# Prelude buffers of a recurrence-and-routing kernel kept to the end, early rows gathered in the prelude, and the first expert search moved

## The chip, the cores and the metric

The kernel runs on one core of a Trainium2 chip. Times are device microseconds (us) of one execution. The kernel before took 1211.76 us as the median of 3 runs (1211.62 to 1213.09). The engines are named as in the profile: PE (matrix products; PEld are its weight loads), DVE (vector engine), ACT (activation engine), POOL (general-purpose engine, which also issues indirect DMAs) and SP (which issues most plain DMAs here).

## The reference, cut to what matters

A gated linear recurrence runs over four sequences of 5056 tokens with 256 channels; its output, 20224 tokens in all, goes through a mixture of 8 experts in which every expert takes exactly N / E = 2528 tokens. Which token goes where is decided greedily over all (token, expert) logits from the largest down.

```python
f = lower_bound + (1 - lower_bound) * sigmoid(f_logit)
h = 0
for t in range(S):
    h = f[:, t] * h + (1 - f[:, t]) * x[:, t]
    y[:, t] = h
x = y.reshape(N, D)                    # N 20224, D 256
logits = x @ w_gate                    # E 8
counts, assigned = zeros(E), -ones(N)
for tok, e in pairs_by_falling_logit(logits):
    if assigned[tok] < 0 and counts[e] < N // E:
        assigned[tok] = e
        counts[e] += 1
for e in range(E):
    m = assigned == e
    out[m] = maximum(x[m] @ w1[e], 0) @ w2[e]     # F 1024
```

## The kernel before, in words

The 20224 tokens are 158 tiles of 128. The program has two stages that share the on-chip memory.

The prelude (lines 147 to 817) takes the tokens in 40 chunks of four tiles (the last has two). For chunk i, `load` (line 161) has SP fetch f_logit and x into tiles `fl` and `xl`; each has four buffers, so a load waits until the chunk four before it has been read. `sig` has ACT form the sigmoid and POOL multiply it with x. `fwd` transposes both on PE (`pf`, `pb`), ACT makes the gate `fg`, DVE runs the scan `g`. `back` (line 714) makes four products `pr` of 264 columns from g with `iw`, a matrix that holds the identity and the gate's weights: 256 columns are the row of the token, 8 its logits. A `pr` tile is one of four PSUM banks and is copied to `hr` by DVE or ACT in turn; POOL copies the logits into `X`. `store` (line 733) has SP write hr (264 columns a token) to `hbuf` in DRAM. `hr` is a ring of 22 buffers; inside the loop a store is issued for every second chunk, at most 18, and the rest when the loads are over.

While the chunks run, `prep` (line 737) finds each token's best expert from X: maximum M, comparison TMP, its product with the numbers `kc`, maximum A, one-hot O; and it forms an integer key K of M and the first-level masks MK of the later search, by comparing K with `thr0_f`. For the first 72 tiles (CE) this is done in three pieces; when it is done, `early` (line 580) estimates from them which expert certainly has 896 rows (EARLY) among these tiles, has POOL load that expert's weights, and lists the ids of those rows. Each step of `early` that needs PE takes a `pr` tile of its own (`ppr.tile`).

The second stage (`moe`, line 912) runs slots -1, 0, ..., 7. Slot -1 is the early expert's first 1920 rows, in chunks of 4, 3, 4 and 4 blocks of 128 rows. For each chunk POOL gathers the rows (`xg <- hbuf, ids`), PE transposes them (`pt`), ACT and DVE split them into a high and a low part (`xh`, `xl`); the weights are split likewise (`w1h`, `w1l`, `w2s`). `first` multiplies one of eight column groups of w1 (six products `pw`), ACT and DVE take hh and hl from it, and `second` multiplies them with w2s (twelve products `py`). ACT copies y, POOL scatters it to `out_dram`. A name that appears twice is meant by its operands: `xl <- fl, xl` is the prelude's product on POOL, `xl <- pt, xh` the low part of gathered rows on DVE.

Between these products the routing runs: `further` lists the other 1024 rows of slot -1, `search` finds a threshold in eight levels, `assign` and `compact` make the lists of the next expert. A planner (class Pace, lines 26 to 100) holds a cost for each operation and fixes at build time in which order the pieces go into PE's, DVE's and ACT's programs; each engine then works its program in order. Helper calls record every operation at line 100, so nearly all rows of the profile have L100 and are told apart by their names; SP's loads have L168 and its stores L735.

The prelude's pools are closed before `moe` opens its own (lines 923 to 938), so that a tile of `moe` lies where prelude tiles lay: one that lies over ring buffers waits until their stores have landed. The order of the pools there (gp for gathered rows, wa1, yp, xp, hp, wb, a gap of 8 KB, wa2) decides which tile lies over which ring buffer: here the first `xl` of gathered rows lies over those of chunks 29 and 31, the second hh over that of chunk 37, the first hl over that of chunk 39.

## Time and profile before

| what | value |
|---|---|
| median of 3 runs | 1211.76 us |
| the profiled execution's own time | 1210.67 us |
| its span, from the first instruction to the last | 1208.9 us |
| mean granted TensorE clock | 0.982 |
| PE busy | 1153.3 us, 95% of the span |
| DVE, ACT, POOL busy | 793.4, 539.0, 461.3 us |
| bytes moved by DMA | 125.25 MB |

A row of a timeline gives the start, the length, the engine, the operation, output and inputs, and in brackets how long the engine had stood idle before it and what ended that. A row of windows gives for a stretch the busy time of PE, PEld, DVE, ACT and POOL (in brackets how many instructions), the granted TensorE clock as a share of full speed, the mean busy share of the DMA engines and the GB/s they moved.

### The profile page before, as it was taken

The numbers are of one execution on the slowest core, as the hardware profiler recorded it, in microseconds if no ns is written. First come the engines' busy times: TensorE is split into PE (matmuls) and PEld (weight loads), VectorE is DVE, ScalarE is ACT, GpSimd is POOL, SyncE is SP. The second block draws the span as 40 slices with busy tenths as digits, with TensorE's granted clock in tenths as the row PEclk, the third lists the DMA queues.
The fourth block names the chain that finished last, engine by engine and source line by source line (L and its number), as shares of the span: only waits on it lengthen the run. The fifth ranks groups of instructions, "written<-read, shape, count | busy, mean of one in ns | idle before, by whom it ended". The sixth has DMA issues, their size and how long they took to land.

```text
span 1208.9 us, 22553 instructions
## 1 busy us (share of the span) xinstructions
PE 1153.3 (95%) x8821; PEld 1048.4 (87%) x8821; DVE 793.4 (66%) x1917; ACT 539.0 (45%) x1104; POOL 461.3 (38%) x459
## 2 busy tenths in 40 slices
PE   7898876998999999999999999999999999999997
PEld 7898865887888988899988988898889989999997
DVE  6998675678767867687887887967744542243221
ACT  7886762326325333643444354222554642253232
POOL 6676560332433333333433433333433333333322
PEclk9999987998999999999999999999999999999999
DMA  9999995112113112211311221111311311131110
GB/s 360 358 330 316 318 334 173 37 54 79 56 49 101 53 41 75 80 48 37 109 48 41 92 63 40 45 41 38 121 45 44 111 47 45 61 106 44 40 35 31
DMA packets 52447, 125.25 MB, mean 104 GB/s; under 512 B 8064, under 2 KB 28288, under 8 KB 51184
## 3 DMA queue, kind: packets, MB, share of 16 engines
q0 software_dynamic: 19248, 60.96, 15.6%
q1 hardware_dynamic: 32544, 62.78, 15.2%
q8 instruction: 71, 1.16, 0.4%
q14 instruction: 40, 0.33, 0.1%
q10 hardware_dynamic: 544, 0.01, 0.0%
HBM read 81.69 MB, written 42.10 MB: 102 GB/s over the span
## 4 chain that ended last, share of the span: by engine, by line
PE 80%; DMA 3%; issue 3%; DVE 1%; POOL 1%; ACT 0%; POOLq 0%; DVEq 0%; SPq 0%; ACTq 0%
PE py L100 37%; PE pw L100 35%; PE rt L100 4%; PE pt L100 2%; DMA hbuf<-hr 1%; PE pr L100 1%; DMA xg<-hbuf,ids 1%; DMA r<-in_moe_w_dram,wi 1%; PE pf L100 1%; PE pb L100 0%; POOL xg L100 0%; POOL out_dram L100 0%; DVE g L100 0%; ACT hh L100 0%; DVE hl L100 0%
## 5 line engine op out<-in xcount | busy, mean ns | idle before, releaser
L100 PE MATMUL py<-w2s,hh 128*128 128x256 f32 x2560 | 490.8, 288 | 0.5 <-ACT y L100 0.5
L100 ACT ACTIVATE hh<-pw 128x512 fp32r<-128x512 f32 (+3 forms) x328 | 191.2, 583 | 553.1 <-PE pw L100 470.8
L100 PEld LDWEIGHTS py<-w2s,hh 128*128 128x128 f32 x2560 | 409.3, 190 | 16.3 <-ACT y L100 0.7
L100 DVE SCALAR_TENSOR_TENSOR hl<-pw,hh 128x512 fp32r<-128x512 f32 (+3 forms) x328 | 219.6, 670 | 232.8 <-ACT hh L100 228.0
L100 PE MATMUL py<-w2s,hl 128*128 128x256 f32 (+1 forms) x1280 | 362.1, 283 | 0.0
L100 POOL DMA_INDIRECT out_dram<-y,ids x160 | 165.1, 1032 | 340.1 <-ACT hh L100 279.9
L100 POOL DMA_INDIRECT xg<-hbuf,ids x160 | 163.6, 1023 | 295.6 <-ACT hh L100 235.9
L100 PE MATMUL pw<-xh,w1h 128*128 128x512 f32 (+3 forms) x656 | 258.3, 394 | 4.7 <-DVE hl L100 4.7
L100 PE MATMUL pw<-xl,w1h 128*128 128x512 f32 (+3 forms) x656 | 259.1, 395 | 0.0
L100 PE MATMUL pw<-xh,w1l 128*128 128x512 f32 (+3 forms) x656 | 256.3, 391 | 0.0
L100 PEld LDWEIGHTS py<-w2s,hl 128*128 128x128 f32 (+1 forms) x1280 | 242.8, 190 | 0.0
L100 PEld LDWEIGHTS pw<-xh,w1l 128*128 128x128 f32 x656 | 124.8, 190 | 22.3
L100 PEld LDWEIGHTS pw<-xh,w1h 128*128 128x128 f32 x656 | 125.6, 191 | 17.2 <-DVE hl L100 5.1
L100 PEld LDWEIGHTS pw<-xl,w1h 128*128 128x128 f32 x656 | 125.6, 191 | 11.3 <-DVE xl L100 0.3
L100 POOL TENSOR_TENSOR xl<-fl,xl 128x1024 f32<-128x1024 f32 (+2 forms) x40 | 92.5, 2312 | 47.1 <-ACT fl L100 36.8
L100 DVE TENSOR_TENSOR_SCAN g<-fg,g,pb 128x512 f32<-128x512 f32 (+4 forms) x78 | 92.9, 1228 | 15.9 <-ACT fg L100 10.7
L100 PE MATMUL pr<-iw,g 128*128 128x136 f32 x632 | 81.8, 281 | 5.6 <-DVE hr L100 5.6
L100 PEld LDWEIGHTS pr<-iw,g 128*128 128x128 f32 x632 | 76.7, 191 | 7.0 <-DVE hr L100 6.8
L100 ACT ACTIVATE junk<-rt,r 128x158 bf16<-128x158 f32 (+1 forms) x153 | 59.4, 389 | 17.3 <-DVE r L100 14.4
L100 DVE TENSOR_TENSOR xl<-pt,xh 128x512 fp32r<-128x512 f32 (+2 forms) x81 | 54.2, 670 | 16.9 <-DMA hbuf<-hr 13.4
L100 PEld LDWEIGHTS pt<-identr,xg 128*128 128x128 f32 x320 | 36.4, 141 | 31.6 <-DVE xl L100 11.5
L100 ACT ACTIVATE fg<-pf,one,nomlb 128x512 f32<-128x512 f32 (+1 forms) x80 | 57.6, 769 | 7.3 <-PE pf L100 5.4
(213 smaller groups left out, 1189.1 us busy)
## 6 DMA issues: line engine op xcount, KB each, us to landing
hbuf<-hr SPq DMA_DIRECT2D x39, 528.0 KB, 9.3
fl<-in_f_logit_dram SPq DMA_DIRECT2D x38, 512.0 KB, 6.4
xl<-in_x_dram SPq DMA_DIRECT2D x38, 512.0 KB, 6.8
xg<-hbuf,ids POOLq DMA_INDIRECT x160, 2.8
out_dram<-y,ids POOLq DMA_INDIRECT x160, 2.4
fl<-in_f_logit_dram SPq DMA_DIRECT2D x3, 256.0 KB, 4.2
xl<-in_x_dram SPq DMA_DIRECT2D x3, 256.0 KB, 4.4
r<-in_moe_w_dram,wi POOLq DMA_INDIRECT x27, 5.5
```

The costliest lines, as they stand in the source:

```text
L100: r = f(*args, **kw)
```

## The change

- The pool of `fl` and `xl` is opened before the prelude's other pools and stays open to the end. A `fl` buffer is now 1056 columns wide (4 rows of 264) instead of 1024; the 32 more columns are zeroed once. In `moe` the `fl` buffers take the place of `gp` and hold gathered rows, the `xl` buffers take the place of `wa1` and hold the split w1 of slot -1 and of the odd slots.
- At the loop's step NCH - 2 the prelude issues the gathers of slot -1's first four blocks; ACT writes the four pieces of its w1h at steps NCH - 2 to NCH. The first of these gathers waits for two of the semaphores of plain DMAs, DMAHW2 and DMAHW5, as the first gather of the kernel before does.
- `early` no longer takes a `pr` tile. `back` gets a job, and the job's products are written into the columns behind 264 of the bank of the chunk's last product. The counts per expert are made by nine products of O with a matrix of ones; the lists are made in pieces of two blocks. `early` has to end inside the loop.
- Keys and first-level masks leave `prep`: the keys are formed for all tiles at once at the search's start, the masks in its first level. `prep` of the tiles up to 136 (CP) now stands inside the loop, and for tiles 72 to 104 the product with kc goes to POOL.
- The bound of 18 stores inside the loop is gone (19 now stand there). The pools of `moe` stand in another order, the gap is gone, and there are 13 y tiles instead of 3.

```diff
-    pre = ExitStack()
-    pin = pre.enter_context(tc.tile_pool(name="pin", bufs=LA))
+    pin = ctx.enter_context(tc.tile_pool(name="pin", bufs=LA))
+    pre = ExitStack()
...
     def early(wi, ids):
-            v.tensor_reduce(CR, O[:, :CE].rearrange("p c e -> p e c"), AX.X, OP.add)
-        yield 'PE'
-        ps = ppr.tile([P, 512], F32, name="pr")
-        nc.tensor.matmul(ps[:, :E], ones_r, CR, start=True, stop=True)
+        def sums(ps):
+            for g in range(CE // 8):
+                nc.tensor.matmul(ps[:, :64], ones_b, O[:, 8 * g:8 * g + 8].rearrange("p c e -> p (c e)"), start=(g == 0),
+                                 stop=(g == CE // 8 - 1))
+        yield sums
+        ps = beside[0]
...
-    def back(i):
+    def back(i, job=None):
...
-            pr = ppr.tile([P, 512], F32, name="pr")[:, :ROW]
+            pr = ppr.tile([P, 512], F32, name="pr")
+            mine = job is not None and k == n - 1
+            if mine:
+                beside[:] = [pr[:, ROW:]]
+                job(beside[0])
+            pr = pr[:, :ROW]
...
     def prep(c0, c1):
-        mb, k1 = m_.bitcast(I32), K1[:, c0:e]
-        far = v if c0 >= CE else nc.gpsimd
+        far = nc.gpsimd if c1 <= 128 else v
...
-        masks(half(K1, 1), thr0_f, c0, c1)
-        yield 'k'
...
+        if i >= NCH - 2:
+            if i < NCH:
+                WSE.append(pin.tile([P, FB, P], F32R, name="xl"))
...
+        if i == NCH - 2:
+            assert stored * KT >= CE
+            XGE = rows_tile(F32R)
+            for q in range(KT):
+                nc.gpsimd.indirect_dma_start(out=XGE[:, q * ROW:(q + 1) * ROW].bitcast(F32), out_offset=None,
+                                             in_=hbuf[:CE * P],
...
-    gp = pool("gp", 3)
-    wa1 = pool("wa1", 1)
-    YB = 3
+    wa2 = pool("wa2", 1)
+    YB = 13
     yp = pool("yp", YB)
+    wb_ = pool("wb", 1)
+    hp = pool("hp", 5)
     xp = pool("xp", 2)
-    hp = pool("hp", 5)
-    wb_ = pool("wb", 1)
-    gap = pool("gap", 1)
...
-    gather(*order[0])
-    issue(4)
+    XG[-1, 0] = g["XGE"].rearrange("p (q r) -> p q r", q=4)
```

PE's program in the middle of the prelude, where `early` has its places; pf, pb and pr are the chunk's products, g_1663 is the 0/1 matrix that picks rows, RAE the list's source, tri and nsub constants:

```order
 L100 MATMUL pf<-ident,fl 128x128 x8
 L100 MATMUL pb<-ident,xl 128x128 x8
-L100 MATMUL pr<-iw,g 128x136 x8
-L100 LDWEIGHTS g_1663
-L100 MATMUL pr<-RAE,g_1663 128x74
+L100 MATMUL pr<-iw,g 128x136 x6
+L100 LDWEIGHTS tri
+L100 MATMUL pr<-ecnt,tri 128x1
+L100 LDWEIGHTS nsub
+L100 MATMUL pr<-RSE,nsub 128x74
+L100 MATMUL pr<-iw,g 128x136 x2
```

Before, the estimate's products stood behind a chunk's eight in a bank of their own; now they stand between the chunk's third and fourth product, in the fourth one's bank.

ACT's program at the border of the two stages, with the semaphores that each row waits for (DMAHW: plain DMAs, DMASW: indirect ones), first before and then after the change; r_227 and r_229 are the raw w2 of slot -1:

```order
L100 ACTIVATE xh<-pt 128x512 [waits DMAHW6_49,DMAHW2_49,PE_49]
L100 ACTIVATE xh<-pt 128x512 [waits PE_49]
L100 ACTIVATE w2s<-r_227 128x2x256 [waits DMAHW4_49,DMAHW3_49,DMAHW5_49,DMASW2_49,DVE_49]
L100 ACTIVATE w2s<-r_227 128x2x256 x3
L100 ACTIVATE hh<-pw 128x512 [waits DMAHW5_49,PE_49]
L100 ACTIVATE hh<-pw 128x512 [waits DMAHW1_49,PE_49,Pool_49]
L100 ACTIVATE hh<-pw 128x512 [waits DMAHW7_49,PE_49]
```

```order
L100 ACTIVATE xh<-pt 128x512 [waits DVE_49,PE_49]
L100 ACTIVATE xh<-pt 128x512 [waits PE_49]
L100 ACTIVATE w2s<-r_229 128x2x256 [waits DMAHW3_49,DMAHW2_49,DMAHW6_49,DMAHW1_49,DMASW2_49]
L100 ACTIVATE w2s<-r_229 128x2x256 x3
L100 ACTIVATE hh<-pw 128x512 [waits DMAHW7_49,PE_49]
L100 ACTIVATE hh<-pw 128x512 [waits DMAHW5_49,DMAHW4_49,PE_49]
L100 ACTIVATE hh<-pw 128x512 [waits PE_49] x3
```

The order of these rows is the same, and the DMAs they wait for are others: w2s now lies over the ring buffers of chunks 22, 26, 29 and 31, the hh tiles over those of chunks 23 to 27, and xh over no ring buffer.

DVE's program at the same place, before and after; w1l's last piece, which is called w1l before and xl after the change (xl<-r_228), stands just ahead of the first row of each:

```order
L100 TENSOR_REDUCE M_160<-X 128x32
L100 TENSOR_TENSOR w2s<-r_227,w2s 128x2x256 [waits DMAHW4_49,DMAHW5_49,DMASW2_49,Activation_49]
L100 TENSOR_TENSOR TMP<-X,M_160 128x256 [waits DVE_49]
L100 TENSOR_SCALAR K_169<-M_160 128x32
L100 TENSOR_TENSOR w2s<-r_227,w2s 128x2x256 [waits Activation_49]
L100 TENSOR_TENSOR TMP<-TMP,kc 128x256 [waits DVE_49]
L100 TENSOR_TENSOR K_169<-K_169,M_160 128x32 [waits DVE_49]
L100 TENSOR_TENSOR w2s<-r_227,w2s 128x2x256 [waits Activation_49]
L100 SCALAR_TENSOR_TENSOR hl<-pw,hh 128x512 [waits DMAHW1_49,DMAHW3_49,Activation_49,Pool_49]
```

```order
L100 TENSOR_REDUCE M_162<-X 128x22 [waits Pool_49]
L100 TENSOR_TENSOR w2s<-r_229,w2s 128x2x256 [waits DMAHW2_49,DMAHW3_49,DMAHW1_49,DMAHW6_49,DMASW2_49,Activation_49]
L100 TENSOR_TENSOR TMP<-X,M_162 128x176 [waits DVE_49]
L100 TENSOR_TENSOR w2s<-r_229,w2s 128x2x256 [waits Activation_49]
L100 TENSOR_TENSOR TMP<-TMP,kc 128x176 [waits DVE_49]
L100 TENSOR_TENSOR w2s<-r_229,w2s 128x2x256 [waits Activation_49]
L100 SCALAR_TENSOR_TENSOR hl<-pw,hh 128x512 [waits DMAHW4_49,Activation_49]
```

The last prep stands between the weight splits with 22 tiles instead of 32 and without its keys K, and the first hl waits for one plain DMA's semaphore instead of two.

## Rows read from the trace of the kernel before

**Rows 1.** The page: the span, and PE's busy time in tenths in 40 equal slices of it.

```profile
span 1208.9 us, 22553 instructions
...
PE   7898876998999999999999999999999999999997
```

**Rows 2.** A window of the second stage (columns as in the section on the profile).

```profile
300.00:500.00 200.00, 199.03 (x1570) 176.66 (x1570) 148.29 (x393) 81.37 (x176) 73.55 (x73) 0.99 0.21 66
```

**Rows 3.** Windows at the border of the two stages.

```profile
172.00:188.00 16.00, 1.47 (x4) 0.73 (x4) 2.56 (x6) 2.05 (x4) 5.55 (x7) 0.53 1.08 356
188.00:195.00 7.00, 6.86 (x22) 5.37 (x22) 5.30 (x13) 3.27 (x6) 0.00 (x0) 0.60 1.10 341
195.00:200.00 5.00, 0.33 (x3) 0.01 (x1) 0.75 (x2) 1.08 (x2) 0.00 (x0) 1.00 0.33 102
```

**Rows 4.** Timelines at the border: DVE, then ACT, then PE.

```profile
187.39 0.69 DVE L100 TENSOR_TENSOR xl<-pt,xh 128x512 fp32r<-128x512 f32 x1 [13.44 <-DMA hbuf<-hr]
...
192.05 0.70 DVE L100 TENSOR_TENSOR w2s<-r,w2s 128x512 fp32r<-128x512 f32 x1
...
194.10 0.70 DVE L100 TENSOR_TENSOR w2s<-r,w2s 128x512 fp32r<-128x512 f32 x1
199.25 0.69 DVE L100 SCALAR_TENSOR_TENSOR hl<-pw,hh 128x512 fp32r<-128x512 f32 x1 [4.44 <-DMA hbuf<-hr]
...
189.42 2.18 ACT L100 ACTIVATE w2s<-r 128x512 fp32r<-128x512 f32 x4
191.61 0.60 ACT L100 ACTIVATE hh<-pw 128x512 fp32r<-128x512 f32 x1
196.87 1.08 ACT L100 ACTIVATE hh<-pw 128x512 fp32r<-128x512 f32 x2 [4.66 <-DMA hbuf<-hr]
...
199.99 0.50 PE L100 MATMUL pw<-xh,w1h 128*128 128x512 f32 x1 [4.67 <-DVE hl L100]
```

**Rows 5.** SP: the last load it issued, its last stores, its stores as a whole, and the page's line on how long a store takes from issue to landing (last column, median).

```profile
154.07 0.47 SPq L168 DMA_DIRECT2D xl<-in_x_dram  x1
...
188.96 3.35 SPq L735 DMA_DIRECT2D hbuf<-hr  x2
...
hbuf<-hr SPq DMA_DIRECT2D x39, 528.0 KB, 9.3
```

**Rows 6.** Windows of the prelude from 36.5 to 167.1 us.

```profile
36.50:51.50 15.00, 15.00 (x136) 14.95 (x135) 14.62 (x30) 13.59 (x24) 11.52 (x10) 1.00 1.04 364
51.50:62.50 11.00, 7.96 (x67) 7.28 (x67) 10.97 (x17) 6.84 (x12) 6.11 (x5) 1.00 0.91 324
62.50:92.70 30.20, 29.39 (x258) 28.74 (x257) 28.65 (x57) 26.28 (x45) 21.98 (x18) 1.00 0.98 338
92.70:110.00 17.30, 14.40 (x113) 14.02 (x112) 13.68 (x31) 11.48 (x20) 10.51 (x10) 0.90 0.82 250
110.00:149.60 39.60, 32.88 (x285) 31.68 (x285) 29.64 (x55) 27.93 (x48) 23.01 (x19) 1.00 0.96 343
149.60:167.10 17.50, 17.50 (x159) 17.37 (x158) 17.35 (x24) 15.19 (x27) 11.63 (x10) 1.00 1.04 314
```

**Rows 7.** PE's largest wait between 36 and 168 us: the waiting product, what it waited for, us in total, times, longest us.

```profile
PE pr L100 <- DVE hr L100: 9.6, 8, 2.3
```

**Rows 8.** Timelines of the prelude: DVE, POOL, and one row of PE.

```profile
53.74 2.84 DVE L100 TENSOR_TENSOR MK<-K,thr0f 128x512 bf16<-128x512 int16 x1
...
86.01 0.69 DVE L100 TENSOR_TENSOR MK<-K,thr0f 128x512 bf16<-128x512 int16 x1
...
93.65 1.22 DVE L100 TENSOR_REDUCE CR<-O 128x8 fp32r<-128x576 bf16 x1
...
152.79 1.50 DVE L100 TENSOR_TENSOR TMP<-X,M 128x256 f32<-128x256 f32 x1
...
53.56 2.48 POOL L100 TENSOR_TENSOR xl<-fl,xl 128x1024 f32<-128x1024 f32 x1 [0.15 <-ACT fl L100]
...
151.64 2.36 POOL L100 TENSOR_TENSOR xl<-fl,xl 128x1024 f32<-128x1024 f32 x1 [1.08 <-ACT fl L100]
...
116.12 0.29 PE L100 MATMUL pr<-RAE,g 128*128 128x74 bf16 x4 [1.15 <-DVE hr L100]
```

**Rows 9.** POOL's timeline at the border: the first gather of slot -1's rows, the fourth, and the last copy of logits; and the page's line on how long a gather takes from issue to landing (last column, median).

```profile
168.82 1.08 POOL L100 DMA_INDIRECT xg<-hbuf,ids  x1 [0.38 <-PE pr L100]
...
173.57 1.15 POOL L100 DMA_INDIRECT xg<-hbuf,ids  x1 [0.30 <-issue]
...
177.33 0.21 POOL L100 COPY X<-hr 128x32 f32<-128x32 f32 x1
...
xg<-hbuf,ids POOLq DMA_INDIRECT x160, 2.8
```

**Rows 10.** Windows of the second stage's start.

```profile
228.00:232.00 4.00, 2.61 (x18) 2.32 (x17) 1.33 (x3) 1.09 (x2) 1.99 (x2) 0.89 0.30 78
232.00:236.00 4.00, 4.00 (x32) 3.84 (x31) 2.20 (x5) 0.49 (x1) 1.00 (x1) 0.68 0.12 34
264.00:276.00 12.00, 10.32 (x72) 8.97 (x70) 7.90 (x25) 4.97 (x7) 2.89 (x3) 1.00 0.48 174
...
292.00:304.00 12.00, 8.47 (x42) 7.40 (x41) 9.77 (x22) 3.85 (x10) 1.11 (x2) 0.72 0.08 23
```

More of the change, by code (lines that the diff above doesn't have):

```diff
@@ L159, in halves, with rows_tile @@
         return ((0, KT // 2), (KT // 2, KT)) if i <= last else ((0, KT),)
+    def rows_tile(dt):
+        return pin.tile([P, KT * ROW], dt, name="fl")
+    rest = []
     def load(i):
         t0, n, np_ = chunks[i]
[L163 removed]
+        both = rows_tile(F32)
+        FT[i] = both[:, :KT * D].rearrange("p (n d) -> p n d", n=KT)
+        if i < LA:
+            rest.append(both[:, KT * D:])
         XT[i] = pin.tile([P, KT, D], F32, name="xl")
@@ new lines, in early @@
+        yield places
+        ps = beside[0]
+        st = ohp.tile([P, len(groups)], F32, name="st")
+        for k in range(2):
+            v.tensor_scalar(st[:, k:k + 1], ps[:, w:w + 1], -512.0 * k, None, op0=OP.add)
+        v.tensor_copy(RAE[:, :w], ps[:, :w])
+        v.tensor_tensor(RAE[:, w - 2:w - 1], ecnt, ps[:, w - 3:w - 2], op=OP.subtract)
+        v.tensor_scalar(elim, ps[:, w:w + 1], -1.0, float(EARLY), op0=OP.mult, op1=OP.add)
+        yield
+        g1 = {}
+        nb = EARLY // P
@@ new lines, in early, with rows @@
+        for b0 in range(0, nb, 2):
+            n = min(2, nb - b0)
+            if b0 % 4 == 0:
+                g1 = ohp.tile([P, 512], BF, name="g1")
+                v.tensor_scalar(g1, IO, st[:, b0 // 4:b0 // 4 + 1], None, op0=OP.is_ge)
+                yield
+            def rows(ps):
+                for b in range(n):
+                    nc.tensor.matmul(ps[:, b * w:(b + 1) * w], g1[:, (b0 + b) % 4 * P:((b0 + b) % 4 + 1) * P],
+                                     RAE[:, :w], start=(b == 0), stop=(b == n - 1), skip_group_check=True)
+            yield rows
+            for _ in blocks(beside[0], b0, n, w, 0, ids[:, b0:b0 + n], False):
+                pass
+            if b0 + n < nb:
+                yield
@@ L629, in further @@
         yield 'DVE',
-        for c in range(104, NT, 32):
-            for _ in prep(c, min(c + 32, NC)):
-                yield 'DVE',
+        for _ in prep(CP, NC):
+            yield 'DVE',
         prog["all"] = True
@@ L988, in split @@
         r1, r2 = RAW[k]
-        one, two = (wa1, wa2) if k % 2 else (wb_, wb_)
-        w1h = one.tile([P, 2, FB, P], F32R, name="w1h")
-        w1l = one.tile([P, 2, FB, P], F32R, name="w1l")
-        w2s = two.tile([P, FB, 2, D], F32R, name="w2s")
+        w1h, w1l = WSE if k < 0 else [], []
+        for t, name in ((w1h, "w1h"), (w1l, "w1l")):
+            for h in range(len(t), 2):
+                t.append(pin.tile([P, FB, P], F32R, name="xl") if k % 2 else
+                         wb_.tile([P, FB, P], F32R, name=f"{name}{h}"))
+        w2s = (wa2 if k % 2 else wb_).tile([P, FB, 2, D], F32R, name="w2s")
         WS[k] = w1h, w1l, w2s
```

151 lines of the change are left out of this document (70 added, 81 removed).

## The prediction

> **What bounds the kernel now.** The page first: PE is busy for nearly the whole span, with dents in the first third and around the sixth and seventh slice [rows 1]. A window of the second stage shows why nothing is to be had behind about 316 us: PE is busy 199.03 of 200 us at a granted clock of 0.99 [rows 2]. The change does not shorten that work, so it can pay only in the dents. There are three of them.
>
> The first is the border of the stages. From 172 to 188 us PE does 1.47 us of work, from 188 to 195 it works at a granted clock of 0.60 (most of it at the lower level, 1.2 GHz, after 16 us with little to do), and from 195 to 200 it does 0.33 us [rows 3]. The timelines name what it waits for: DVE's xl waited 13.44 us, until 187.39, for a store of ring rows, ACT's second hh until 196.87 for another, DVE's first hl until 199.25 for a third; then PE resumes for good at 199.99 [rows 4]. SP issued its last load at 154.07 and the last two stores in a piece from 188.96 to 192.3, each landing some 9.3 us after its issue [rows 5], while the DMA engines were full (share 1.08 to 1.10 until 195) [rows 3].
>
> The second is the prelude itself. In the quiet stretches PE is busy 15.00 of 15.00 and 17.50 of 17.50 us; in between 7.96 of 11.00, 29.39 of 30.20, 14.40 of 17.30 and 32.88 of 39.60 [rows 6]. The largest named wait there is that of pr for hr, 9.6 us in eight pieces [rows 7]. The third is the start of the second stage, with PE at 2.61 of 4.00 and the next 4 us at clock 0.68, and two later holes [rows 10].
>
> **The border.** The rows of w2s, hh and hl now lie over other ring buffers: w2s over chunks 22, 26, 29 and 31, hh over 23 to 27. The xl of gathered rows lies over none; its wait goes, and ACT's first w2s waits in its place for the same store of chunk 31. I call its landing T0, 187.39 us now [rows 4]. Behind the waiting w2s stand, on ACT, its three fellows and all hh, and on DVE the low parts of w2s and then hl. From T0, ACT needs 2.18 us for the four w2s, then hh begins; DVE starts its first low part about 0.55 us after T0 (a quarter of 2.18), the third 2.05 us later (192.05 to 194.10, with pieces of a prep between, as after the change), and hl 0.60 us behind that; from the start of hl to PE's resumption 0.74 us pass (199.25 to 199.99) [rows 4]. By ACT: 2.18 + 0.60 (a whole hh) + 0.74 = 3.5 us; by DVE: 0.55 + 2.05 + 0.60 + 0.74 = 3.9 us. DVE is last: PE resumes at 191.3 where it was 199.99, 8.7 us earlier, and at the same place in its work, since only the three products that fit the free banks stand ahead in both. I take **-8.6 us**. The bounds are 0 (something still waits for the last store) and -9.1 (ACT's path).
>
> The gathers of the first four blocks, which ended their issues at about 174.7 [rows 9], move ahead of the last copy of logits, and the four w1h of ACT into the prelude. Both lay beside the wait for T0 before and do so after, so I cost them at nothing; if T0 came before 175 they would be the cover that is gone. POOL's last copy of logits stands behind five gathers (it was at 177.33 behind six [rows 9]); DVE's first reduction at the border waits for it.
>
> **The prelude, on PE's side.** The lost time is 3.04 + 0.81 + 2.90 + 6.72 = 13.5 us of idle PE, and the clock of 0.90 over 17.3 us costs another 1.7 [rows 6]: 15.2 us. Of this the estimate's own pr tile explains the 9.6 us of waits for hr: it holds one of four banks until DVE has read it, and the chunk's products queue for three. With its products beside the fourth, no bank is lost. The mask operation at 53.74 took 2.84 us where its fellow took 0.69 [rows 8]; it leaves the prelude, which is worth 2.1 us. The sum of O on DVE, 1.22 us, becomes nine small products on PE; the nearest row, four of 74 columns in 0.29 us [rows 8], makes them 0.7 us once, hidden or not too small to matter. Left is 15.2 - 9.6 - 2.1 = 3.5 us, which I let stand: DVE is busy 14.62 of 15.00 us in a quiet stretch [rows 6], so the estimate's and prep's remaining pieces still push the scans of some chunks, and they now include the tiles from 104 to 136. PE's side gives 11.7 us.
>
> **The prelude, on the DMA side.** T0 comes when a fixed number of bytes has passed. SP's order of loads and stores stays; one store more stands in the loop. Where PE never waits, the DMA share is 1.04; in the disturbed stretches 0.91, 0.98, 0.82 and 0.96 [rows 6]. Filled up to 1.04 they give 0.13 x 11.0 + 0.06 x 30.2 + 0.22 x 17.3 + 0.08 x 39.6 = 10.2, by 1.04 that is 9.8 us. Both sides have to give; each stretch gives only the smaller of the two, so the sum is below 9.8. I take **-8 us**. The ends are 0 (the transfers are already as dense as these loads and stores allow) and -15.2 (all PE time, if the drain runs at the border's 1.10). The store's issues move with the loads, so T0 moves by the same 8.
>
> The row on the locked operation is worth a second look. The mask at 53.74 ran while POOL's product at 53.56 ran, and ended just behind it (56.04); the comparison TMP at 152.79 took 1.50 us for 256 columns, ending just behind POOL's product from 151.64 to 154.00, where a mask of 512 columns took 0.69 alone [rows 8]. The Trainium skill, "SBUF — State Buffer", section "Who interferes with whom", says that a VectorE instruction with two inputs in SBUF and a GpSimd instruction that reads SBUF use one shared port pair, exclusively, so that one blocks until the other is through; these two rows agree. It speaks against this change in one point: TMP stays in the prelude for every prep, one of them moves in from the second stage, and another prep's product with kc is put on POOL. By that rule three such TMPs may lose 0.8 us each (1.50 - 0.69), PE's side would give 9.3 instead of 11.7, and the prelude some 7.5 instead of 8.
>
> **Behind the border.** At 228 to 236 PE loses 1.39 us idle, 0.11 x 2.61 = 0.3 and 0.32 x 4.00 = 1.3 us of clock [rows 10], 3.0 together: the gather of late rows is not there in time. The list that it needs (further, without its preps) comes one step of PE earlier in the new order. A step of 18 products is some 18 x 199 / 1570 = 2.3 us [rows 2], less than the loss, and the gathers still go out 1.6 us apart (168.82 to 173.57 for four [rows 9]); I take half, **-1.5 us**, ends 0 and -3.0. The keys and masks that return to DVE at the search's start are beside full PE work (DVE 148.29 of 200 us busy in the second stage [rows 2]): nothing; if the search's end came late, slot 0's border would pay. The hole at 264 to 276 (weights after the routing's result) and the one at 292 to 304 [rows 10] have what they wait for moved by less than a step, so 0, within 3 us either way.
>
> **The sum.** -8.6 - 8 - 1.5 = -18.1 us. The profiled execution took 1210.67 us, its span 1208.9 and 1.8 around it, which stays. That makes 1192.6; the median of the runs stands 1.1 us above the profiled execution, so 1193.7.
>
> **Rivals.**
>
> The transfers set the prelude (B): the loads and stores are already as dense as they can be, the PE waits only hide behind them, and T0 stays at 187.4. For it: shares of 0.96 and 0.98 over 70 us, against it 0.82 over 17 us with PE idle [rows 6]. Then -8.6 - 1.5, and 1201.7.
>
> Everything goes (C): all 15.2 us of the prelude and all 3.0 behind the border. For it: the bytes drain at 1.10 rather than 1.04 at the border [rows 3]. Against it: DVE's fill. -8.6 - 15.2 - 3.0 = -26.8, and 1185.0.
>
> The change does not do at the border what it says (D): a hl or hh still lies over a late store, and PE resumes only when the last has landed. The waits in the order name semaphores, not stores. Then -8 - 1.5, and 1202.3; if the prelude gives nothing either, -1.5, and 1210.3, which is no change.
>
> The early gather waits for every store (E, slower): the first gather now stands in the prelude and waits for two DMA semaphores; if their counts stand for late stores, it starts only when the last has landed, at about 199.1. The four gathers then issue until 205 (168.82 to 174.72 now is 5.9 [rows 9]), the rows land 2.8 us later [rows 9] and are split in 0.7 (xl's 0.69 [rows 4]), 208.5, and the three products that were done by 195 are still to do, some 6.6 us at the clock of that stretch (6.86 with a few transposes [rows 3]): 8.5 + 6.6 = 15.1 us later than 199.99. 15.1 - 8 - 1.5 = +5.6, and 1217.4. It decides from a first gather later than some 190. Against it: the gather before waited on the same two and started at 168.82, 0.38 us after its releaser on PE [rows 9].
>
> **How the numbers follow.** Forecast 0.60, B 0.17, C 0.13, D 0.06 (half of it with the prelude's gain), E 0.04. About 0.2%, 2.4 us, is what a measurement of this kernel can tell from no change. Faster: 0.60 + 0.17 + 0.13 + 0.03 = 0.93; same 0.03 (the half of D without the prelude); slower 0.04. The range of 1185 to 1204 takes in the forecast's own spread (prelude 4 to 11, behind the border -3 to +3), B and most of C and D.
>
> **What would show it.** At the border: no DVE row xl <- pt, xh with a wait for hbuf; ACT's first w2s released by a store, PE's pw some 3.9 us behind it at about 183, and no hh or hl released by a store. In the prelude: no pr <- hr waits of 1 us and more, no mask rows, SP's last load at about 146 instead of 154.07. The PE share between 228 and 236, moved with the rest, up by half of its loss. Wrong would be the forecast if the last load stands where it stood (B), or if PE's resumption follows the last store (D), or if POOL's first gather starts late (E).

## The result

The changed kernel takes 1194.5 us (median of 4 runs, 1192.13 to 1195.04), the kernel before 1212.33 in the same series; the ratio is 0.9849, with a 95% interval of 0.9832 to 0.9866. The forecast was 1193.7 in a range of 1185 to 1204. The profiled execution took 1195.04, the slowest of the four, with a span of 1193.3; against the profiled one of before that is 15.6 us less.

The page after, to be held against [rows 1]: the span and PE's busy tenths.

```profile
span 1193.3 us, 22554 instructions
...
PE   8999978999999999999999999999999999999997
```

The dents in the first third are nearly gone, the one at the border (sixth slice) is smaller. The windows of the prelude after, beside [rows 6]:

```profile
51.50:62.50 11.00, 10.62 (x94) 10.32 (x94) 11.00 (x20) 9.47 (x16) 7.04 (x6) 1.00 1.02 357
62.50:92.70 30.20, 27.55 (x238) 26.45 (x237) 27.31 (x47) 24.52 (x43) 21.45 (x17) 1.00 0.97 348
92.70:110.00 17.30, 15.89 (x131) 15.61 (x132) 15.29 (x26) 12.06 (x21) 9.32 (x9) 0.90 0.77 239
110.00:149.60 39.60, 38.39 (x338) 37.26 (x337) 37.21 (x69) 33.25 (x57) 29.71 (x24) 1.00 1.04 393
```

PE's idle time between 110 and 149.6 fell from 6.7 us to 1.2, that from 51.5 to 62.5 from 3.0 to 0.4; but from 62.5 to 92.7 it rose from 0.8 to 2.7, and from 92.7 to 110 the granted clock is 0.90 as before. Together they are 5.7 us idle where 13.5 were.

The timelines at the border after, in the order of [rows 4]: DVE, ACT, PE, and ahead of them SP's last load (154.07 in [rows 5]).

```profile
147.00 0.47 SPq L176 DMA_DIRECT2D xl<-in_x_dram  x1
...
173.65 0.69 DVE L100 TENSOR_TENSOR xl<-pt,xh 128x512 fp32r<-128x512 f32 x1 [6.00 <-ACT xh L100]
...
181.11 0.69 DVE L100 TENSOR_TENSOR w2s<-r,w2s 128x512 fp32r<-128x512 f32 x1 [2.75 <-ACT w2s L100]
...
183.43 0.68 DVE L100 SCALAR_TENSOR_TENSOR hl<-pw,hh 128x512 fp32r<-128x512 f32 x1
...
180.45 2.19 ACT L100 ACTIVATE w2s<-r 128x512 fp32r<-128x512 f32 x4 [4.67 <-DMA hbuf<-hr]
182.54 1.55 ACT L100 ACTIVATE hh<-pw 128x512 fp32r<-128x512 f32 x3
...
184.17 0.73 PE L100 MATMUL pw<-xh,xl 128*128 128x512 f32 x1 [3.64 <-DVE hl L100]
```

The xl of gathered rows waits for ACT's xh and no more for a store; ACT's first w2s is the one operation on ACT, DVE or PE that a store releases here, at 180.45 (POOL's first gather, at 162.11, had waited 0.71 us for one); hh and hl follow without a wait of their own, and PE resumes 3.72 us behind w2s. Before, 12.60 us passed from the landing of the same store (187.39) to PE's resumption (199.99).

### The profile page after: what moved, and what is told of

It is laid out like the page before. It is cut to its first block, busy times and chain, and to the rows that moved or that the text cites. A ratio compares the mean times of both kernels' runs of the same rounds, so it can differ in the third digit from the quotient of the medians.

```text
span 1193.3 us, 22554 instructions
## 1 busy us (share of the span) xinstructions
PE 1153.3 (97%) x8829; PEld 1049.4 (88%) x8829; DVE 791.0 (66%) x1905; ACT 540.8 (45%) x1104; POOL 459.2 (38%) x463
## 5 line engine op out<-in xcount | busy, mean ns | idle before, releaser
L100 POOL DMA_INDIRECT fl<-hbuf,ids x160 | 161.7, 1011 | 297.9 <-ACT hh L100 246.7
L100 PE MATMUL pw<-xh,xl 128*128 128x512 f32 (+3 forms) x672 | 232.2, 388 | 3.6 <-DVE hl L100 3.6
L100 PEld LDWEIGHTS pw<-xh,xl 128*128 128x128 f32 x672 | 125.7, 190 | 21.0 <-DVE hl L100 4.1
L100 PE MATMUL pw<-xl 128*128 128x512 f32 (+3 forms) x336 | 131.0, 390 | 0.0
L100 PE MATMUL pw<-xh,w1h 128*128 128x512 f32 (+1 forms) x320 | 126.5, 395 | 0.0
L100 PE MATMUL pw<-xl,w1h 128*128 128x512 f32 (+1 forms) x320 | 126.4, 395 | 0.0
L100 PE MATMUL pw<-xh,w1l 128*128 128x512 f32 (+1 forms) x320 | 125.5, 392 | 0.0
L100 PEld LDWEIGHTS pw<-xh,w1l 128*128 128x128 f32 x320 | 60.2, 188 | 11.7
L100 PEld LDWEIGHTS pw<-xl 128*128 128x128 f32 x336 | 64.0, 190 | 6.0 <-DVE xl L100 0.3
L100 PEld LDWEIGHTS pw<-xh,w1h 128*128 128x128 f32 x320 | 60.7, 190 | 6.2
```

Source lines behind the costliest of these rows:

```text
L100: r = f(*args, **kw)
```

## The experiments

Their times come from four other series, in which the kernel before had medians of 1211.35 to 1212.4 us; a difference of less than some 2 us from 1194.5 is not told apart from none. The same holds of SP's last load: in the change and in the runs below called w2s last, needed stores first and gathers at the second stage's start, the programs of PE and SP are the same up to it, and it stands at 147.00, 147.66, 145.42 and 146.81 us. "First w2s" is the start of ACT's first w2s at the border, the landing of chunk 31's store where a store releases it.

### The estimate

Old estimate: `early` and its calls as in the kernel before, all else as changed.

```diff
     def early(wi, ids):
...
-        yield sums
-        ps = beside[0]
...
+        yield 'PE'
+        ps = ppr.tile([P, 512], F32, name="pr")
+        nc.tensor.matmul(ps[:, :E], ones_r, CR, start=True, stop=True)
...
-        job = next(est, None) if est is not None else None
+        due = next(est, None) if est is not None else None
...
+        if due == 'PE':
+            next(est)
```

> The changed kernel with the whole estimate of the kernel before in it: own pr banks, the reduction of O on DVE, pieces of four and three blocks. The run with an own bank but short pieces moved the last load by 2.5 us and the first w2s by 0.9 only. Theory (a bank is lost for as long as DVE takes to read it; pieces of four blocks hold it over some four chunks): waits of pr for hr of 7 to 10 us return, the last load stands at 151.5 to 154 and ACT's first w2s at 183 to 187; the time is 1197 to 1201. Rival (transfers set the landing): last load late as above, but first w2s under 182.5, and the time within 2 us of 1194.5. Then the 7 us by which the landing moved come from something else than the estimate and the masks.

Measured: 1205.41 us (1204.08 to 1206.28), ratio to before 0.9943 (0.9927 to 0.996): 10.9 us slower than the change. PE's waits between 36 and 160 us with two of the eight (a product of the estimate and one of a later chunk), and then SP's last load, ACT's first w2s and PE's resumption from its timelines:

```profile
PE pr L100 <- DVE hr L100: 10.1, 8, 2.0
...
117.12 0.29 PE L100 MATMUL pr<-RAE,g 128*128 128x74 bf16 x4 [1.16 <-DVE hr L100]
...
126.63 0.73 PE L100 MATMUL pr<-iw,g 128*128 128x136 f32 x4 [1.09 <-DVE hr L100]
```

```profile
155.06 0.56 SPq L176 DMA_DIRECT2D xl<-in_x_dram  x1
...
188.51 2.19 ACT L100 ACTIVATE w2s<-r 128x512 fp32r<-128x512 f32 x4 [5.30 <-DMA hbuf<-hr]
...
192.22 0.80 PE L100 MATMUL pw<-xh,xl 128*128 128x512 f32 x1 [4.30 <-DVE hl L100]
```

The eight waits of [rows 7] are back (there 9.6 us), and last load, landing and resumption each stand 8.1 us later than after the change. So all that the change gained in the prelude came from the estimate. The theory held in kind; last load, landing and time all went beyond its ranges (the time by 4.4 us). Of the 10.9 us, 8.1 stand at PE's resumption; the other 2.8 come behind it, and the windows from 20 to 80 us behind the resumption, of the change and then of this run, show them:

```profile
204.17:264.17 60.00, 56.64 (x487) 50.26 (x484) 42.84 (x125) 23.16 (x48) 17.82 (x18) 1.00 0.21 69
```

```profile
212.22:272.22 60.00, 56.45 (x458) 50.12 (x455) 40.19 (x118) 19.98 (x39) 17.26 (x17) 0.94 0.21 69
```

PE is idle for almost the same time in both, but the granted clock is 0.94 instead of 1.00 over 56.45 us of work, which is 3.4 us.

Old estimate, read at once: the same, but DVE reads a piece's bank in one go.

```diff
-            for m, _ in enumerate(blocks(ps, 4 * k, n, w, 0, ids[:, 4 * k:4 * k + n], False)):
-                if m % 2 == 0:
-                    yield 'DVE'
+            for _ in blocks(ps, 4 * k, n, w, 0, ids[:, 4 * k:4 * k + n], False):
+                pass
```

> The changed kernel with the whole estimate of the kernel before (own banks, pieces of four and three blocks), as in the run that was 11 us slower, but with DVE reading each piece's bank in one go instead of a block or two a chunk. Theory (the cost is a bank held over several chunks: waits of 1.1 to 1.2 us at each chunk from 117 to 145): five waits become two or three, the last load comes from 155.1 to 150 or 152, the time from 1205.4 to 1198 to 1202. Rival (own banks cost the same for a short hold, or the reduction of 1.2 us and the longer pieces on DVE are what costs): within 2 us of 1205.4.

Measured: 1197.83 us (1195.76 to 1199.99), 7.6 us below the run with the old estimate. The same views of it:

```profile
PE pr L100 <- DVE hr L100: 5.4, 4, 1.9
```

```profile
149.09 0.47 SPq L176 DMA_DIRECT2D xl<-in_x_dram  x1
...
181.88 2.19 ACT L100 ACTIVATE w2s<-r 128x512 fp32r<-128x512 f32 x4 [4.66 <-DMA hbuf<-hr]
```

Four waits instead of eight, all four of the estimate's own products; the chunks' products wait no more. A bank that is read within a chunk costs one wait; a bank that DVE reads over several chunks costs one at each of them. Last load and time came a little earlier than expected (150 to 152, 1198 to 1202), and four waits were left where two or three were expected; the theory held. The 3.3 us that are left to the change were not taken apart.

Own bank: the estimate in its new form (pieces of two blocks, read at once), with a bank of its own.

```diff
-            if mine:
-                beside[:] = [pr[:, ROW:]]
-                job(beside[0])
...
+        if job is not None:
+            beside[:] = [ppr.tile([P, 512], F32, name="pr")]
+            job(beside[0])
```

> The changed kernel with one thing undone: the estimate's products take a pr bank of their own again, behind the chunk's four. Theory (the bank): each of the six pieces of products holds one of four banks until DVE has read it, so PE's waits of pr for hr return, 1.1 to 1.2 us each (9.6 us in 8 before the change), 6 to 7 us together; SP's last load moves from 147.0 to 152 or later, and the time goes from 1194.5 to 1199 to 1201. Rival (transfers set the prelude): the waits return, but the last load stays within 1.5 us of 147.0 and the time within 2 us of 1194.5. Second rival (DVE's operations locked by POOL are what is left of the prelude's loss): the bank's waits fall into the stalls that are there anyway, and half or less comes back, 1196 to 1198.

Measured: 1194.87 us (1193.84 to 1196.31), no difference. The waits of pr for hr were 4.6 us in six, the last load stood at 149.46 (2.5 later), but the first w2s at 181.32 (0.9 later). The theory missed the time; the rival named the waits' return without an effect, and with a load 2.5 instead of 1.5 us late it came nearer. Between the two forms of the estimate it is thus the length for which a bank is held, and less whose bank it is, that made most of the difference. The new place forces the short form, since two blocks of 74 columns fit behind the 264 of a bank's 512 and four do not.

### What is left in the prelude

The changed kernel's rows at 84 and 90 us, DVE and then POOL, where the loss of the second window rose:

```profile
84.31 2.31 DVE L100 TENSOR_TENSOR TMP<-X,M 128x64 f32<-128x64 f32 x1
...
90.21 2.11 DVE L100 TENSOR_TENSOR O<-kc,A 128x64 bf16<-128x64 f32 x1
...
84.17 2.36 POOL L100 TENSOR_TENSOR xl<-fl,xl 128x1024 f32<-128x1024 f32 x1
...
89.88 2.36 POOL L100 TENSOR_TENSOR xl<-fl,xl 128x1024 f32<-128x1024 f32 x1
```

TMP of 64 columns starts 0.14 us behind POOL's product and ends 0.09 us behind its end (86.62 and 86.53); O meets the next product in the same way. Prep earlier: its steps stand ahead of the chunk's hr copies.

```diff
+        prep_step(99 if i == NCH else 3 if done == CE and upto < CE + 8 else PS if done < CE else 1 + (i > NCH - 3))
         if i >= 1:
             back(i - 1, job)
...
-        prep_step(99 if i == NCH else 3 if done == CE and upto < CE + 8 else PS if done < CE else 1 + (i > NCH - 3))
```

> The changed kernel with each step of prep issued before the chunk's hr copies instead of behind them, so that DVE's two-input operations TMP and O fall where POOL waits for hr and runs no product. Theory (lock): TMP and O, which took 2.31, 2.11, 1.80, 1.00 and 1.49 us, take 0.2 to 0.65 each; 7 us of DVE go, the last load moves from 147.0 to 142 to 145, and since the transfers set when chunk 31 has landed, PE's resumption and the end gain 1 to 4 us: 1190.5 to 1193.5. Rival (these stalls are hidden by the transfers altogether): the operations get short, the time stays within 1 us of 1194.5. Rival that speaks against it: the hr copies come later and PE waits for a bank (waits of pr for hr appear), and it is slower.

Measured: 1192.37 us (1186.87 to 1192.67), ratio to before 0.9824 (0.9798 to 0.985). DVE and POOL in that run:

```profile
85.86 0.22 DVE L100 TENSOR_TENSOR TMP<-X,M 128x64 f32<-128x64 f32 x1
...
119.12 2.28 DVE L100 TENSOR_TENSOR TMP<-X,M 128x256 f32<-128x256 f32 x1
...
83.05 2.36 POOL L100 TENSOR_TENSOR xl<-fl,xl 128x1024 f32<-128x1024 f32 x1
```

The same operation takes 0.22 us when it starts behind POOL's product (85.41), a tenth of 2.31. But others now fell into a product: 2.28 at 119.12, where the change had 1.80. Between 40 and 165 us all TMP and O on DVE take 11.1 us together, in the change 11.5: the edit moved the stalls and took hardly any of them away. PE waited for hr again, 2.1 us in three pieces, as the last rival said. The last load came 2.1 us earlier (144.93), the first w2s 2.3 (178.16), PE's resumption 2.3 (181.88), the time 2.1 by the medians, which is about what runs with the same prelude differ by; one run of four lay 5 us lower, and why isn't known. So the theory holds in each operation, but what these stalls cost in time is not shown.

The Trainium skill, "SBUF — State Buffer", section "Who interferes with whom", gives the rule that the prediction weighed (one port pair for a two-input VectorE instruction and a GpSimd one that reads SBUF, held for a whole instruction); the 2.31 and 0.22 us of the same operation agree with it.

### The keys and masks

Keys in prep: the keys and first-level masks stand in `prep` again, those of the tiles up to 136 in the prelude.

```diff
         v.tensor_tensor(t_, x_, bcl(m_, e - c0), op=OP.is_ge)
+        v.tensor_scalar(k1, mb, 31, 0x7FFFFFFF, op0=OP.arith_shift_right, op1=OP.bitwise_and)
...
+        v.tensor_tensor(k1, k1, mb, op=OP.bitwise_xor)
...
+        masks(half(K1, 1), thr0_f, c0, c1)
+        yield 'k'
...
         if first:
-            yield from first_keys()
```

> The changed kernel with the keys and first-level masks back in prep, for the tiles up to 136 in the prelude. Theory (lock): a mask that meets POOL's product waits for its end; of four masks of 0.28 to 0.69 us some two take 2 to 3 us, the last load moves 2 to 5 us later, the time is 1196.5 to 1200. Rival (only the operations' own lengths count): masks of 0.69, 0.69, 0.28 and 0.69 us and the keys come to some 3 us on DVE, spread over four chunks, of which DVE's room takes most; the last load moves by under 1.5 us and the time is 1194 to 1196. If the keys' return to DVE behind the border cost anything, the time goes below 1194.

Measured: 1186.56 us (1186.46 to 1187.21), ratio to before 0.9795 (0.9779 to 0.9811): 7.9 us faster than the change, which both expected times missed; the last sentence foresaw the direction. Timelines of DVE, ACT and POOL in that run, and POOL's row of the change itself:

```profile
55.13 2.84 DVE L100 TENSOR_TENSOR MK<-K,thr0f 128x512 bf16<-128x512 int16 x1
...
90.88 0.21 DVE L100 TENSOR_TENSOR TMP<-X,M 128x64 f32<-128x64 f32 x1
...
179.23 2.19 ACT L100 ACTIVATE w2s<-r 128x512 fp32r<-128x512 f32 x4 [3.73 <-DMA hbuf<-hr]
...
240.41 0.99 POOL L100 DMA_INDIRECT r<-in_moe_w_dram,wi  x1 [5.88 <-ACT hh L100]
```

```profile
248.34 0.99 POOL L100 DMA_INDIRECT r<-in_moe_w_dram,wi  x1 [6.27 <-ACT hh L100]
```

In the prelude the masks cost nothing that can be told: the mask of [rows 8] is stalled again (2.84 us), but with it the later operations stand elsewhere against POOL's products, TMP takes 0.21 instead of 2.31 us, and the last load comes at 146.69 instead of 147.00. The gain lies behind the border: from PE's resumption to the end of the span the change takes 1009.1 us, this run 1001.7. The search's result is needed for slot 0's weights: POOL asks for them 57.3 us behind PE's resumption (183.13) instead of 64.2. It begins earlier too: the first threshold TH on DVE stands 16.3 us behind the resumption in the change and 10.4 in this run (16.2 in the kernel before). The row of before, of the change and of this run:

```profile
216.15 0.29 DVE L100 SCALAR_TENSOR_TENSOR TH<-rt,PRE 128x128 int16<-128x128 f32 x1 [0.80 <-PE rt L100]
```

```profile
200.51 0.29 DVE L100 SCALAR_TENSOR_TENSOR TH<-rt,PRE 128x128 int16<-128x128 f32 x1 [1.40 <-PE rt L100]
```

```profile
193.57 0.28 DVE L100 SCALAR_TENSOR_TENSOR TH<-rt,PRE 128x128 int16<-128x128 f32 x1
```

The windows behind the border of the change and then of this run show where PE gets that back; the first row of each is the first 200 us behind the resumption as a whole:

```profile
184.17:384.17 200.00, 191.64 (x1512) 169.90 (x1513) 142.82 (x394) 79.18 (x182) 62.16 (x61) 0.98 0.21 68
...
212.00:216.00 4.00, 2.77 (x21) 2.38 (x20) 3.07 (x6) 1.09 (x2) 2.12 (x3) 1.00 0.26 72
252.00:260.00 8.00, 5.87 (x40) 4.92 (x39) 5.63 (x13) 6.30 (x11) 0.00 (x0) 1.00 0.52 195
...
272.00:280.00 8.00, 5.39 (x30) 4.68 (x29) 5.48 (x14) 2.69 (x6) 2.24 (x3) 0.79 0.20 53
318.00:322.00 4.00, 2.72 (x33) 2.24 (x30) 0.95 (x6) 1.19 (x2) 2.49 (x3) 1.00 0.35 88
```

```profile
183.13:383.13 200.00, 195.37 (x1560) 174.51 (x1561) 153.14 (x411) 81.45 (x186) 69.29 (x65) 1.00 0.22 70
...
212.00:216.00 4.00, 4.00 (x31) 3.96 (x31) 3.86 (x9) 1.06 (x3) 1.36 (x2) 1.00 0.25 63
...
246.00:250.00 4.00, 2.31 (x17) 1.79 (x17) 3.29 (x8) 3.46 (x5) 1.02 (x1) 1.00 0.77 310
266.00:270.00 4.00, 1.41 (x11) 1.27 (x12) 2.75 (x6) 1.33 (x3) 2.05 (x2) 1.00 0.23 61
318.00:322.00 4.00, 4.00 (x30) 3.53 (x28) 3.83 (x10) 1.09 (x2) 1.77 (x2) 1.00 0.09 33
```

The change loses 1.23 + 2.13 + 2.61 + 1.28 = 7.3 us of PE in four holes, and has the clock at 0.79 in one of them; the run with the keys in prep loses 1.69 + 2.59 = 4.3 in two, at full clock. Over the 200 us it is 8.4 us idle at a clock of 0.98 against 4.6 at 1.00, so 3.7 us of the gain are idle time and the rest, some 4 us (0.02 x 191.64), is clock.

Keys without masks: only the keys stand in prep, the masks stay at the search's start.

```diff
+        v.tensor_scalar(k1, mb, 31, 0x7FFFFFFF, op0=OP.arith_shift_right, op1=OP.bitwise_and)
...
+        v.tensor_tensor(k1, k1, mb, op=OP.bitwise_xor)
...
-        v.tensor_scalar(k1, mb, 31, 0x7FFFFFFF, op0=OP.arith_shift_right, op1=OP.bitwise_and)
-        v.tensor_tensor(k1, k1, mb, op=OP.bitwise_xor)
         yield 'DVE',
```

> The changed kernel with the keys K formed in prep again, but the first-level masks left at the search's start. The run with both back was 8 us faster, and nearly all of that came behind the border: the weights of slot 0 were asked for 57.3 us behind PE's resumption instead of 64.2. Theory (the search is one chain, and each DVE operation at its head, keys 0.6 and masks 1.6 us, moves all of it): the keys' share is a quarter to a third, weights 61.5 to 63 us behind the resumption, the time 1191 to 1193.5. Rival (the order of the pieces, in which the keys stand behind the last prep and the masks behind them, costs a whole step of PE): all or nothing, so 1187 or 1194.5.

Measured: 1192.58 us (1190.45 to 1194.22). POOL asks for the weights at 247.17, 61.5 us behind PE's resumption at 185.71 (the last load stood 2.2 us later than in the change, at 149.20, and took back part). The first TH (199.01) stands 13.3 us behind the resumption, between the 16.3 and 10.4 above. The keys' share is 2.7 of 6.9 us in the chain of the search, more than the third of the theory, and 1.9 of 7.9 in the time, a little under its quarter and hardly more than these runs tell apart. All or nothing, as the rival had it, is not what the chain shows.

### The border

w2s last: two pools exchanged, so that w2s lies over the buffers of chunks 37 and 39.

```diff
-    wa2 = pool("wa2", 1)
     YB = 13
     yp = pool("yp", YB)
+    wa2 = pool("wa2", 1)
```

> The changed kernel with two pools exchanged, so that slot -1's w2s lies over the ring buffers of chunks 37 and 39 instead of 22, 26, 29 and 31; nothing else moves in PE's program. Theory (the landing of the store under w2s sets PE's resumption, 3.7 us behind it): ACT's first w2s waits until the last store has landed, about 189.5 (the DMA engines are full until then), PE resumes at 193.2 instead of 184.2, and the time is 1194.5 + 9 = 1203.5 (1201 to 1205). Rival (the resumption hangs on the gathers and splits, or what is lost here is given back behind the border): under 3 us slower.

Measured: 1205.55 us (1204.95 to 1206.08), 11 us slower, 0.6 beyond the theory's range. ACT and PE:

```profile
191.45 2.19 ACT L100 ACTIVATE w2s<-r 128x512 fp32r<-128x512 f32 x4 [15.36 <-DMA hbuf<-hr]
...
195.17 0.79 PE L100 MATMUL pw<-xh,xl 128*128 128x512 f32 x1 [13.76 <-DVE hl L100]
```

Again 3.72 us from w2s to PE; resumption and time both 11 us later. What the store under w2s costs at the border passes to the end one for one.

Needed stores first: the stores over whose buffers w2s, hh and hl lie go out first behind the last load.

```diff
-    for i in range(stored, NCH):
+    soon = [22, 26, 29, 31, 27, 25, 24, 23]
+    for i in soon + [i for i in range(stored, NCH) if i not in soon]:
         store(i)
```

> The changed kernel with the stores behind the last load in another order: those of chunks 22, 26, 29, 31, 27, 25, 24 and 23, over whose buffers w2s, hh and hl lie, come first. Theory (PE's resumption hangs on chunk 31's store alone): ACT's first w2s is no longer released by a store but runs behind xh at about 176; PE's wait of pw for hl (3.6 us) goes and the three first products run into the rest; 3 to 5 us faster, 1189.5 to 1191.5. Rival (all stores' bytes have to be through, in whatever order, since the DMA engines are full): the same wait, within 1 us of 1194.5. A second rival: the gathers of slot -1's first rows, which were served between stores, get slower, and the gain is 0 to 2 us.

Measured: 1189.48 us (1189.06 to 1190.12), ratio to before 0.9819 (0.9803 to 0.9836). ACT's w2s:

```profile
174.07 2.17 ACT L100 ACTIVATE w2s<-r 128x512 fp32r<-128x512 f32 x4
```

No store releases it any more, it runs on behind xh, and PE's wait of pw for hl is gone. 5 us, as the theory had it, though 1.6 of the 6.0 us between the two profiled executions stand already at the last load (145.42 instead of 147.00), ahead of the place of the edit. The DMA engines had the same bytes to move; their order alone took the wait away.

Gathers at the second stage's start: the first four are issued there, as before.

```diff
-            XGE = rows_tile(F32R)
-            for q in range(KT):
-                nc.gpsimd.indirect_dma_start(out=XGE[:, q * ROW:(q + 1) * ROW].bitcast(F32), out_offset=None,
...
-    XG[-1, 0] = g["XGE"].rearrange("p (q r) -> p q r", q=4)
-    asked[-1, 0] = 0
+    gather(*order[0])
+    issue(4)
```

> The changed kernel with the gathers of slot -1's first four blocks issued at the second stage's start again, behind POOL's last copy of logits, instead of in the prelude. Theory (they lie beside the wait for chunk 31's store, cost nothing and bring nothing): xh and xl some 1 to 3 us later, ACT's first w2s still released by the store at 180 to 181, the time within 1.5 us of 1194.5. Rival (without the early gathers the splits come behind the store's landing): ACT's w2s stands behind xh in its order, so every us by which xh comes later than 180 is lost; then 1197 or more.

Measured: 1196.03 us (1193.17 to 1197.57): no difference that can be told. The expected place was wrong. POOL's program put these gathers behind one copy of logits instead of two; the first was issued at 158.92 and not at 162.11, and xh came earlier:

```profile
169.88 0.60 ACT L100 ACTIVATE xh<-pt 128x512 fp32r<-128x512 f32 x1 [2.68 <-PE pt L100]
...
179.88 2.19 ACT L100 ACTIVATE w2s<-r 128x512 fp32r<-128x512 f32 x4 [7.24 <-DMA hbuf<-hr]
```

In the change xh stood at 173.02. The earlier xh brought nothing, since the store under w2s came later in both.

### Together

Keys and order: keys and masks in prep, needed stores first.

```diff
+        masks(half(K1, 1), thr0_f, c0, c1)
...
+    for i in soon + [i for i in range(stored, NCH) if i not in soon]:
```

> The changed kernel with both edits that were faster by themselves: keys and first-level masks in prep (1186.6 instead of 1194.5) and the stores over whose buffers w2s, hh and hl lie first (1189.5). Theory (two different places, the routing behind the border and the wait for chunk 31): they add up but for the wait of 2.3 us that is left at the border in the first of them, so 1186.6 - 3 to 5 = 1181.5 to 1183.5. Rival (both remove the same wait in turn): 1186 to 1187.

Measured: 1184.96 us (1183.23 to 1185.29). Neither the theory's range nor the rival's: 1.6 us below the run with the keys alone. In that run PE had waited only 2.26 us for hl (3.64 in the change), so less was left for the order of the stores to gain. With prep earlier as well:

```diff
+        prep_step(99 if i == NCH else 3 if done == CE and upto < CE + 8 else PS if done < CE else 1 + (i > NCH - 3))
         if i >= 1:
             back(i - 1, job)
```

> The same with prep's steps before the hr copies too. Theory (lock): the mask of 2.84 us and TMP and O of 1.7 to 1.9 us fall to 0.7 and less; with the wait for stores gone, PE's resumption follows the prelude's end and the gathers behind it, so the 4 to 6 us that DVE gets back in the prelude count: 2 to 5 us below the run without it, 1177 to 1181. Rival (the gathers of slot -1's first rows are served late because the queues are full of stores): within 1.5 us of the run without it.

Measured: 1186.31 us (1184.22 to 1189.21), within 1.5 us of the run without it, as the rival said: xh stood at 172.98 there and at 172.19 without, and ahead of it PE's transposes waited for gathered rows in both. But the theory was not put to the test. The mask fell from 2.84 to 0.68 us, while TMP at 44 us rose from 0.52 to 1.31, TMP at 75 from 0.65 to 1.40, and O at 131 from 0.62 to 1.79, and the last load moved by 0.4 us only (145.35 and 145.78).

With the late gathers instead:

```diff
+        masks(half(K1, 1), thr0_f, c0, c1)
...
+    for i in soon + [i for i in range(stored, NCH) if i not in soon]:
...
+    gather(*order[0])
+    issue(4)
```

> The three edits that were not slower by themselves, together: keys and first-level masks in prep, the needed stores first, and the first gathers issued at the second stage's start (where POOL put them 3 us earlier than in the changed kernel, and xh came at 169.9 instead of 173.0). Theory (with no store left to wait for, PE's resumption hangs on the gathered rows, and 2 to 3 us of gathers count): 1182 to 1183.5 instead of 1185.0. Rival (something else ends last at the border): within 1 us of 1185.0.

Measured: 1182.59 us (1181.16 to 1183.01), ratio to before 0.9753 (0.9737 to 0.9769): 11.9 us below the changed kernel, the fastest of all. PE's resumption:

```profile
177.68 0.50 PE L100 MATMUL pw<-xh,xl 128*128 128x512 f32 x1 [0.42 <-DVE hl L100]
```

ACT's xh stood at 169.25, 2.9 us earlier than with the early gathers. The place of the gathers, which brought nothing as long as a store was last, brings 2.4 us once it is not.

## Why the prediction was right, and where it was not

The time was inside the range and 0.8 us from the forecast, of the likeliest case and not of a rival; that it came so near is in part luck, since behind the border errors of 7.4 and 5.7 us stand against each other. The terms, in the profiled executions:

| term | forecast | measured |
|---|---|---|
| prelude, by the landing of chunk 31 | -8 | 187.39 to 180.45: -6.9 |
| border, from that landing to PE's resumption | -8.6 | 12.60 to 3.72: -8.9 |
| behind the border | -1.5 | -15.6 at the end, -15.8 at the resumption: +0.2 |
| together | -18.1 | -15.6 (medians of the runs: -17.8) |

**The border** was right in mechanism and size: the same store, its four w2s, three low parts, hl and PE, 3.9 us forecast and 3.72 found; in the other kernels of this table it is 3.71 to 3.72 and once 3.90 (from first w2s to PE). Rival D fell with it, since no hh or hl waits for a store, and rival E with POOL's first gather, which started at 162.11.

| kernel | last load | first w2s | PE resumes |
|---|---|---|---|
| changed | 147.00 | 180.45 | 184.17 |
| old estimate | 155.06 | 188.51 | 192.22 |
| old estimate, read at once | 149.09 | 181.88 | 185.60 |
| own bank | 149.46 | 181.32 | 185.04 |
| keys in prep | 146.69 | 179.23 | 183.13 |
| prep earlier | 144.93 | 178.16 | 181.88 |

**The prelude on PE's side** was right in its first part. The estimate's bank was worth 8.1 us at the landing, what was taken for the whole prelude, not all of the 9.6 in waits; in time it was worth 10.9, and the 2.8 us between come behind the border, as a lower clock. The words "holds one of four banks until DVE has read it" were the right ones, but the credit went to the wrong half of the edit: the place beside a product matters little (own bank: +0.4 us), that each piece is read within a chunk matters most (7.6 of 10.9 us). In the four windows shown with the result PE's idle time fell by 7.8 us, where the forecast had 11.7 for PE's side.

**The mask's 2.1 us** was the step that failed in the prelude. The lock on DVE did not go with the mask; TMP and O fell into it, 2.31 and 2.11 us. With the masks back the last load was as early as without. The paragraph on the lock had the mechanism, and its price of 0.8 us for each TMP was too low by more than half for the worst one (2.31 against 0.22); it also set TMP of 256 columns against a mask of 0.69 us, where TMP itself takes 0.42 when nothing stalls it (at 46.36 after the change). What an operation loses depends on how much of POOL's product is left when it starts, up to nearly all of 2.36.

**The prelude on the DMA side**: the last load moved by 7.1 and the landing by 6.9 us. Rival B, that the transfers hold the landing where it is, fell; by the table above the landing follows the last load by 32 to 33.5 us. In the run with an own bank it followed by 31.9, so part of that delay was caught up; what catches it up was not settled.

**Behind the border** two steps failed. One is "The keys and masks that return to DVE at the search's start are beside full PE work [...]: nothing". They are the head of the chain of the search, which sets slot 0's weights and rows, and cost 7.4 us there (1009.1 us from PE's resumption to the end, against 1001.7 with both in prep); the forecast named this way of failing, "if the search's end came late", and gave it no price. The other is the -1.5 us with its ends of 0 and -3.0: the kernel before takes 1008.9 us from the resumption to the end, so the rest of the change was worth 7.2 us behind the border, nearly five times what was forecast. That it is the prep of the tiles from 104 to 136, which no longer stands between resumption and search, is likely by the rows of TH (16.2 us behind the resumption before, 10.4 with keys and masks in prep), but no run undoes it alone. -7.2 and +7.4 make the +0.2 of the table; that it lies only 1.7 us from the forecast is luck, an error of 5.7 us against one of 7.4. Not tested by themselves are also prep's product with kc on POOL, the 19th store and the 13 y tiles.

The list of late rows, on which the -1.5 us were built, did not come a step earlier in the change: POOL's first gather of them stands 19.2 us behind the resumption before, 19.0 in the change and 17.1 with keys and masks in prep. The hole at 228 still shrank a little (1.39 us and a clock of 0.68 behind it [rows 10] became 1.23 at full clock), the one at 292 too (3.53 us to 2.61), that at 264 did not (2.08 us from 260 to 280 before; 2.13 between 252 and 260 after), and a new one of 1.28 stands at 318. In products done, the change was ahead for a while: the 600th product py of the second stage starts 178.9 us behind the resumption before and 176.3 in the change. At the 3120th, 833.4 us behind it in both, that is gone; one more hole (1.12 us between 344 and 384) took part of it, and why the rest went while PE was never idle is not known.

Against the profiled executions the forecast's sum was 2.5 us too large. That the median came out 0.8 us from it owes something to the runs' spread: the profiled execution of the change lies 0.5 us above its median, that of the kernel before 1.7 below the median of the same series.

## What to carry to other kernels

A short product that borrows one of a few banks costs a wait at every stage of the pipeline for as long as it holds it: read it at once; whose bank it is mattered little here. An operation off the busy engine is not free when it is the head of a chain: look for what waits for the chain's end, not for what runs beside the operation. Where a stage begins over the buffers of the last one, lay its first tiles over those whose stores go out first, or send those stores first.

## What was not expected of the hardware

- One and the same DVE operation (two inputs, 64 columns) took 2.31 us when it started just behind a POOL product of 2.36 us and 0.22 us when it started just behind its end; the stall moved from operation to operation as the order changed, and removing the stalled one did not remove it.
- The granted clock did not fall with each hole: in the change it stayed 1.00 with 1.23 us of PE idle in 212 to 216 and 2.13 in 252 to 260, and was 0.79 in 272 to 280 with 2.61; with keys and masks in prep it stayed 1.00 with 2.59 idle in 266 to 270. Before, 1.39 idle at 228 was followed by a clock of 0.68 [rows 10].
